# Chunks 6 to 13 of an RWKV-7 scan inverted in blocks of 32 steps and joined on TensorE, with the schedule around it moved

## The chip, the cores and the metric

The kernel runs on one core of a Trainium2 chip. The metric is the device time of one launch in microseconds. Every time given is a median over runs or comes from one profiled execution, and the text says which. The engines are named as the profile names them: PE is the matmul engine and PEld its weight loads, DVE is VectorE, ACT is ScalarE, POOL is GpSimd, SP the engine whose queue issues most DMAs.

## The reference

An RWKV-7 state recurrence over 768 steps, for 4 batches of 8 heads with 40 dimensions each, and on its output a feed-forward layer with a squared ReLU:

```python
for t in range(S):                                   # S = 768
    y[:, :, t] = np.einsum('bhd,bhde->bhe', rt, state)
    Sa = np.einsum('bhde,bhe->bhd', state, at)
    state_decay = state * wt[:, :, None, :] - np.einsum('bhd,bhe->bhde', Sa, bt)
    state = state_decay + np.einsum('bhd,bhe->bhde', vt, kt)
x = y.transpose(0, 2, 1, 3).reshape(B * S, H * D)    # 3072 x 320
h = np.maximum(x @ w_in, 0.0)                        # w_in 320 x 2048
out = h * h @ w_out                                  # w_out 2048 x 320
```

The FFN weights arrive as 64-bit floats; the kernel turns them into 32-bit ones itself.

## The kernel before

The sequence is cut into 24 chunks of 128 steps: chunk i is batch i mod 4, steps 128 (i div 4) onward. A chunk i needs the state that chunk i-4 left, so the chunks form one long sequence with four interleaved chains. Inside a chunk, all steps are solved together, which needs the inverse of a unit lower triangular matrix for each head. A chunk's 128 steps are two halves of 64, and for each half and head a 64 x 64 matrix is inverted; the coupling between the halves is done later with N (`g["N"]`).

The work on a chunk comes in parts, each a Python generator that issues a few instructions and yields:

- `early(i)`, five steps: w, b and a are loaded, turned on PE, the running products of the decay are made on DVE (scans, two reciprocals), b and a are scaled, and their products for all pairs of steps are made on PE. ACT copies these into `N`, and the blocks to be inverted go to DRAM (`kept_q` or `kept_d`, `kept_n`, `kept_m`), with the decays (`kept_e`).
- the inversion, on POOL: `take` loads the blocks of a *unit* of chunks, one block to a partition, and `solve` runs the forward substitution, two POOL instructions a step (L443 and L445). The result goes to DRAM (`kept_t`). Units hold 1, 1, 2, 2, 2, 2, 4, 4, 4 and 2 chunks. Units 0 to 3 (chunks 0 to 5) are "fine": each 64 x 64 matrix is given as two 32 x 32 blocks, 31 steps, and the block below the diagonal is computed on PE. Units 4 to 9 run 63 steps on whole halves.
- `inverses(i)` fetches a chunk's result into the tile `T`. For a coarse unit that is only a load. For a fine one it is the *join*: DVE turns the blocks (`upper_`), ACT spreads them over `T` with the mask `which`, PE makes 16 small products into `mv`, ACT copies them, PE makes 16 more, ACT copies these into `T`. The tiles for this (`mv`, `turned`, `joins`) lie at the end of the FFN's `hidden` buffer, which is free then.
- `rest(i)`, nine steps or more: k, r and v are turned, the masked products A and RV made, the state is brought up to date, and it drives `inverses(i)`.
- `chain(i)`, eleven steps: the part that needs the state of the chunk four before; it ends in a third of a token tile.
- `ffn()`: for each group of three chunks eight up-projection steps (6 matmuls each) and twelve out-projection steps, 160 in all.
- `rounding()`: the pieces of the weights, 10 for the up-projection and 16 for the other, each a few operations on ACT and DVE, out of staging room that lies in `w_out` and in the first 4608 words of `hidden`.

The order on every engine is the order in which the program issues, written out by hand. The start (L750 to L792) prepares chunks 0 to 3. Then come 24 *slots*. Slot i interleaves, in twelve steps (`weave`), chain(i), some steps of the FFN (`share`), the early parts listed for the slot in `ahead`, rest(i+1), and in slots 0 to 4 pieces of weights (`pieces_in`, the number and the step by which they end). What is left of a generator after the twelve steps is issued in one go (`run`), rest last. When all chunks of a unit have had their early part, `take` and `solve` of the unit are issued to POOL at the end of the slot. Unit 4 is stopped after 33 of its 63 steps, and the first part of unit 5's data is loaded before it goes on (`AHEAD`, `EARLIER`).

The schedule before, in numbers: early parts 4 and 5 in slot 0, 6 and 7 in slot 1, 8 and 9 in slot 2, 10 in slot 3, 11 in slot 4, 12 and 13 in slot 5, then one a slot, 17 and 18 in slot 9. The FFN takes 5 steps in slot 4, from its fourth step on, and then up to 7 a slot.

`soon(i)` tells whether the load for chunk i is issued early in `rest(i)`, or late, because its unit has only just been solved:

```python
soon = lambda i: i < 2 * B or unit_of[i - 1] == unit_of[i]      # B = 4
```

Of the kernel before, what the change touches and what calls it, by code (L numbers as in the profile page):

```python
# [17 lines left out]
def kernel(  # L18
# [22 lines left out]
    nc = tc.nc  # L41
# [4 lines left out]
    C = 128  # L46
# [122 lines left out]
    more_rings()  # L169
    x_ = loaded[0] = {nm: fetch(nm, src, 0) for nm, src in (("k", k), ("r", r))}  # L170

    which = single("which", [128, 2])
    nc.gpsimd.memset(which, 0.0)
    for n in range(4):
        nc.gpsimd.memset(which[n * 32:(n + 1) * 32, n % 2:n % 2 + 1], 1.0)

    whole = lambda t_: t_

# [114 lines left out]
    Q = HC // 2  # L293
    kept_e = [dram.tile([USED, 3, NP, C + 2], FP32, tag=f"e{i}", name=f"kept_e{i}") for i in range(len(order))]

    sizes = [1, 1] + [2] * 4 + [4] * ((len(order) - 12) // 4) + [2]
    units = [(sum(sizes[:u]), n) for u, n in enumerate(sizes)]

    FINE = 4
    SMALL = units[FINE][0]  # L300
    kept_q = dram.tile([SMALL, H, 2, 2, Q, Q], FP32, tag="q", name="kept_q")
    kept_m = [dram.tile([2, Q, H, Q], FP32, tag=f"m{i}", name=f"kept_m{i}") for i in range(SMALL)]
# [31 lines left out]
    turned = lambda nm, bufs: new(nm, [128, NP, 128], bufs)  # L334


    def spare(name, i):
        at = NF * GB * C - (("mv", "turned", "joins").index(name) * 2 + i % 2 + 1) * H * Q
        return free_words[:, at:at + H * Q].rearrange("p (h t) -> p h t", h=H)

    def early(i, g=None):

# [43 lines left out]
        if g is None:  # L386
            store(kept_n[i], t_[:HC, :, HC:], 1)
        else:
            g["dec"], g["N"] = dec, new("N21", [HC, H, HC], 2)
            nc.scalar.copy(g["N"], t_[:HC, :, HC:])  # L390
            g["joins"] = spare("joins", i)
            for half in range(2):
                nc.scalar.copy(g["joins"][half * HC:half * HC + Q], joins(half))
        yield
# [5 lines left out]

    part_of = lambda u: given[:, u % 3 * Q * Q:(u % 3 + 1) * Q * Q] if u < FINE else given


    EARLIER = Q * HC

    def take(u, queues, words=slice(None)):
        first, nb = units[u]
        if u < FINE:
            kept = kept_q[first:first + nb].rearrange("b h f k s t -> (b h f k) (s t)")
        else:  # L410
            kept = kept_d[u].rearrange("b h f w -> (b h f) w")
        cols = classes(u)
        rows = 128 // cols
        for col in range(cols):
            queues[col % len(queues)].dma_start(out=part_of(u)[col * rows:(col + 1) * rows, words], in_=kept[:, words])  # L415

    def solve(u, between={}):
        run(solving(u, between))

    def solving(u, between={}, stop=None):  # L420

        first, nb = units[u]
        fine = u < FINE
        size = Q if fine else HC
        cols = classes(u)
        rows = 128 // cols
        part = part_of(u)
        words = size // cols * size
        at = u * Q * Q // 2 if fine else 0
        ts = solved[:, at:at + words]  # L430
        nc.gpsimd.memset(ts, 0.0)
        for col in range(cols):
            nc.gpsimd.memset(ts[col * rows:(col + 1) * rows, col::size + cols], -1.0)
        t3 = ts.rearrange("p (j t) -> p j t", t=size)
        for s in range(size - 1):
            if s in between:
                between[s]()
            if s == stop:
                yield
            n, m_ = s // cols + 1, size - 1 - s  # L440
            at = s * size + s + 1 if s < Q else Q * HC + (s - Q) * (Q + 1) + 1
            p_ = new("half_p", [128, 528], 1)[:, :n * m_].rearrange("p (j t) -> p j t", j=n)
            nc.gpsimd.tensor_tensor(p_, part[:, at:at + m_].unsqueeze(1).to_broadcast([128, n, m_]),  # L443
                                    t3[:, :n, s:s + 1].to_broadcast([128, n, m_]), Alu.mult)
            nc.gpsimd.tensor_tensor(t3[:, :n, s + 1:], t3[:, :n, s + 1:], p_, Alu.subtract)  # L445
        to = kept_t[u]
        to = to.rearrange("n b h f k j t -> (n b h f k) (j t)") if fine else to.rearrange("n b h f j t -> (n b h f) (j t)")
        nc.gpsimd.dma_start(out=to, in_=ts)
# [3 lines left out]
    def inverses(i, g, queue=nc.sync):  # L452
# [13 lines left out]
        if "N" not in g:  # L466
            g["N"] = new("N21", [HC, H, HC], 2)
            queue.dma_start(out=g["N"], in_=kept_n[i])
            if u < FINE:
                g["joins"] = spare("joins", i)  # L470
                for half in range(2):
                    queue.dma_start(out=g["joins"][half * HC:half * HC + Q], in_=kept_m[i][half])
        if u >= FINE:
            return
        yield
        upper_ = spare("turned", i)
        nc.vector.transpose(upper_.rearrange("p h t -> p (h t)"), blocks.rearrange("p h t -> p (h t)"))
        for n in range(2):
            nc.scalar.activation(T[:, :, n * Q:(n + 1) * Q], blocks, Act.Copy, scale=which[:, n:n + 1])
        yield  # L480
        small = lambda: psum(ps_w)[:, :H * Q].rearrange("p (h t) -> p h t", h=H)
        p_ = small()
        mv = spare("mv", i)
        ends_ = [(slice(half * HC, half * HC + Q), slice(half * HC + Q, (half + 1) * HC)) for half in range(2)]
        for h in range(H):
            for one, two in ends_:
                mm(p_[two, h], g["joins"][one, h], upper_[one, h], True)
# [175 lines left out]
    def ffn():  # L663
        for gi in range(len(order) // GB):
# [1 line left out]
                yield False  # L666
            t_ = tokens.pop(gi)
            hid = []
            for f in range(0, NF, 2):
                square(hid[-2:])  # L670
                ps = [psum(ps_f if gi < len(order) // GB - 1 else ps_w)[:, :GB * C] for _ in range(2)]
                for e, p_ in enumerate(ps):
                    half = slice(e * DP, (e + 1) * DP)
                    mm(p_, w_third[half, f * 64:f * 64 + 128], t_[half, NT, :], True)
# [10 lines left out]
            for n in range(GB):  # L685
                bb, c = order[gi * GB + n]
                p_ = psum(ps_f if gi < len(order) // GB - 1 else ps_w)[:, :DM]
                for f in range(NF):
                    mm(p_, hid[f][:, n * C:(n + 1) * C], w_out[:, f], f == 0)
                    if f % PART == PART - 1 and f < NF - 1:  # L690
                        yield True
                o_ = new("o", [128, DM], 2)
# [10 lines left out]
    def run(gen):  # L703
        for _ in gen:
            tick()
# [87 lines left out]


    TOTAL = 12
    ahead = {0: (4, 5), 1: (6, 7), 2: (8, 9), 3: (10,), 4: (11,), 5: (12, 13)}
    ahead.update({i: (i + 8,) for i in range(6, 9)})
    ahead[9] = (17, 18)
    ahead.update({i: (i + 9,) for i in range(10, len(order) - 9)})

    PER, LAG = NF // 2 + 4 * GB, 3
    by_then = [0] * B + [5]
    for i in range(B + 1, len(order)):
        by_then.append(min(by_then[-1] + 7, PER * (i + 1) // GB - PER - LAG if i > 2 * B else PER * i))
    share = {i: (n - (by_then[i - 1] if i else 0), 4 if i == B else 0) for i, n in enumerate(by_then)}
    pieces_in = {0: (4, TOTAL), 1: (6, TOTAL), 2: (6, TOTAL), 3: (7, TOTAL), B: (4, 4)}
    done = set(range(B))
    unit = unit_of[B]

    AHEAD, under_way = (FINE,), []  # L810
    for i in range(len(order)):
        bb, c = order[i]
        n, begin = share[i]
# [16 lines left out]
        weave(*jobs)  # L830
        while unit < len(units) and all(m_ in done for m_ in range(len(order)) if unit_of[m_] == unit):
            flush()
            if under_way:

                take(unit, own, slice(0, EARLIER))
                run(under_way.pop())
                take(unit, own, slice(EARLIER, Q * (HC + Q)))
            else:
                take(unit, own)
            if unit in AHEAD:  # L840
                under_way.append(solving(unit, stop=Q + 1))
                next(under_way[0])
            else:
                solve(unit)
            unit += 1
    flush()
    run(second)
# [30 lines left out]
```

## Time and profile before

| | us |
|---|---|
| median of three runs (lowest, highest) | 1046.84 (1044.67, 1049.31) |
| the profiled execution | 1047.3 |
| its span, from the first to the last instruction | 1045.6 |
| PE busy in the span | 927.4 (89%) |
| POOL busy | 670.6 (64%) |
| DVE busy | 496.8 (48%) |
| ACT busy | 273.0 (26%) |
| mean granted clock of PE | 0.915 of full speed |

The groups of instructions that the change touches, from the profile's list by line, engine and tiles (count, busy us in all, mean ns of one, idle us just before them):

| group | count | busy | mean | idle before |
|---|---|---|---|---|
| POOL L443, product of a step of the substitution | 502 | 298.9 | 595 | 90.2 |
| POOL L445, its subtraction | 502 | 322.4 | 642 | 39.3 |
| PE, first products of the join (into `mv`) | 192 | 5.6 | 222 | 16.6 |
| PE, second products of the join | 192 | 7.3 | 223 | 9.2 |
| ACT L479, blocks spread over T | 12 | 5.4 | 500 | 22.6 |
| ACT L489, copies of mv | 12 | 4.4 | 363 | 1.1 |
| ACT L496, copies into T | 12 | 4.3 | 360 | 5.7 |
| DVE L477, blocks turned | 6 | 2.6 | 438 | 23.4 |

POOL stores the units' results to `kept_t` at 49.0, 76.3, 107.9, 148.0, 251.4, 338.8, 475.1, 609.8, 747.8 and 844.2 us.

How to read it: a stretch of the span is told by the engines' busy time in it. Matmuls are pipelined and their ends modelled, so a PE that is busy is not one at its peak, while a gap on PE is a real wait. "PEclk" is the share of its clock that PE was granted. A releaser is what the waiting instruction's semaphore was last raised by.

### The profile page before, as it was taken

What the parts mean: (1) busy time and instruction counts of PE and PEld (TensorE: products, weight loads), DVE (VectorE), ACT (ScalarE), POOL (GpSimd) and SP (SyncE); (2) the same over time, 40 slices, a digit from 0 to 9 for tenths busy, and PEclk for the clock granted to TensorE, in tenths of its full rate; (3) what the DMA queues carried; (4) which work ended last, traced back from release to release, by engine and by line L of the source; (5) the groups of instructions that cost most, each with busy time, mean ns of one, the idle gap of its engine ahead of it and who ended that gap; (6) DMA issues with size and microseconds to landing.
All of it is one profiled execution on the core that took longest, in us unless ns stands there. A gap on an engine that the chain in (4) does not pass through costs nothing.

```text
span 1045.6 us, 19803 instructions
## 1 busy us (share of the span) xinstructions
PE 927.4 (89%) x7824; PEld 672.1 (64%) x7824; DVE 496.8 (48%) x940; ACT 273.0 (26%) x627; POOL 670.6 (64%) x1128
## 2 busy tenths in 40 slices
PE   6364665688999999997999999999999999999998
PEld 5253455576667766775677766775677567756656
DVE  5556685796554465453744545534432432222120
ACT  3132332334332133122232132113212311232020
POOL 4778454897898599995999949999668820000000
PEclk8656676667999999998999999999999999999999
DMA  8987989688184938198564596064425432520000
GB/s 108 154 145 146 178 196 179 163 158 147 43 137 92 193 55 136 24 164 194 61 113 90 87 183 119 21 118 59 115 50 98 66 72 49 98 30 7 23 0 19
DMA packets 260360, 106.92 MB, mean 102 GB/s; under 512 B 243724, under 2 KB 249356, under 8 KB 258604
## 3 DMA queue, kind: packets, MB, share of 16 engines
q1 hardware_dynamic: 255740, 86.65, 47.8%
q0 software_dynamic: 3440, 18.88, 7.8%
q8 instruction: 62, 1.02, 0.4%
q10 hardware_dynamic: 1088, 0.13, 0.1%
q14 instruction: 30, 0.25, 0.1%
HBM read 72.47 MB, written 31.19 MB: 99 GB/s over the span
## 4 chain that ended last, share of the span: by engine, by line
PE 52%; POOL 28%; DMA 10%; issue 5%; DVE 2%; ACT 2%; SPq 1%; POOLq 0%; DVEq 0%; ACTq 0%
PE ps_f L87 26%; POOL half_t L445 14%; POOL half_p L443 13%; PE ps_w L87 11%; PE ps_c L87 10%; DMA half_n<-kept_d 3%; PE ps_w L314 2%; DMA kept_t<-half_t 1%; DMA half_n<-kept_q 1%; DMA in_w<-in_w_dram 1%; DMA T<-kept_t 1%; DMA w_out<-in_moe_w_in_dram 1%; PE ps_w L542 1%; DMA kept_m<-N 1%; POOL half_n L415 1%
## 5 line engine op out<-in xcount | busy, mean ns | idle before, releaser
L443 POOL TENSOR_TENSOR half_p<-half_n,half_t 128x70 f32<-128x70 f32 (+52 forms) x502 | 298.9, 595 | 90.2 <-DMA half_n<-kept_d 39.8
L445 POOL TENSOR_TENSOR half_t<-half_t,half_p 128x70 f32<-128x70 f32 (+52 forms) x502 | 322.4, 642 | 39.3
L87 PE MATMUL ps_f<-w_out,hid 128*128 128x320 f32 x672 | 198.6, 440 | 0.0
L87 PE MATMUL ps_f<-tokens,w_in 128*128 128x384 f32 x448 | 162.3, 506 | 0.0
L661 DVE TENSOR_TENSOR hid<-hid 128x384 f32<-128x384 f32 x128 | 94.4, 752 | 139.4 <-ACT hid L679 139.0
L87 PEld LDWEIGHTS ps_f<-w_out,hid 128*128 128x128 f32 x672 | 121.6, 190 | 44.9 <-issue 2.1
L87 PEld LDWEIGHTS ps_f<-tokens,w_in 128*128 128x128 f32 x448 | 82.1, 193 | 77.2 <-issue 33.8
L679 ACT ACTIVATE hid<-ps_f 128x384 f32<-128x384 f32 x112 | 54.9, 490 | 201.1 <-PE ps_f L87 201.1
L330 DVE TENSOR_TENSOR A<-ps_w,upper 128x512 f32<-128x512 f32 x48 | 30.9, 686 | 108.0 <-PE ps_w L87 108.0
L87 PE MATMUL ps_w<-decay,bT 40*128 40x128 f32 x352 | 31.7, 330 | 33.2 <-DVE decay L360 29.5
L514 DVE TENSOR_TENSOR kvT<-ps_w,dec 128x512 f32<-128x512 f32 x24 | 16.5, 687 | 88.7 <-DMA dec<-kept_e 46.6
L87 PE MATMUL ps_f<-tokens,w_third 64*128 64x384 f32 x224 | 55.4, 540 | 0.0
L87 PEld LDWEIGHTS ps_w<-decay,bT 40*128 40x128 f32 x352 | 26.9, 229 | 41.8 <-DVE decay L360 26.7
L87 PE MATMUL ps_c<-xr,T 64*64 64x40 f32 x768 | 39.1, 242 | 13.7 <-ACT xr L592 6.7
L351 DVE TENSOR_TENSOR_SCAN decay<-ps_w,ones 128x64 f32<-128x64 f32 x88 | 23.8, 270 | 54.2 <-PE ps_w L314 54.1
L87 PEld LDWEIGHTS ps_c<-xr,T 64*64 64x64 f32 x768 | 32.5, 148 | 25.1 <-ACT xr L592 13.1
L330 DVE TENSOR_TENSOR RX<-ps_w,upper 128x512 f32<-128x512 f32 x48 | 30.8, 683 | 26.2 <-PE ps_w L87 25.9
L330 DVE TENSOR_TENSOR RV<-ps_w,upper 128x512 f32<-128x512 f32 x48 | 30.9, 686 | 18.1 <-PE ps_w L87 17.9
L355 DVE RECIPROCAL decay<-decay 128x256 f32<-128x256 f32 x22 | 38.3, 1739 | 0.0
L356 DVE RECIPROCAL decay<-decay 128x256 f32<-128x256 f32 x22 | 37.3, 1694 | 0.0
L87 PE MATMUL ps_w<-rT,xnT 40*128 40x128 f32 x384 | 34.2, 293 | 2.4 <-ACT rT L524 2.4
L524 ACT COPY rT<-ps_w 128x512 f32<-128x512 f32 x24 | 14.0, 585 | 82.5 <-PE ps_w L314 82.5
(139 smaller groups left out, 1391.0 us busy)
## 6 DMA issues: line engine op xcount, KB each, us to landing
kept_e<-decay SPq DMA_DIRECT2D x22, 633.8 KB
dec<-kept_e SPq DMA_DIRECT2D x22, 633.8 KB
hid<-in_moe_w_out_dram SPq DMA_DIRECT2D x16, 320.0 KB
half_n<-kept_d POOLq DMA_DIRECT2D x6, 768.0 KB, 11.4
in_w<-in_w_dram SPq DMA_DIRECT2D x24, 160.0 KB
in_ab<-in_b_dram SPq DMA_DIRECT2D x24, 160.0 KB
in_ab<-in_a_dram SPq DMA_DIRECT2D x24, 160.0 KB
in_k<-in_k_dram SPq DMA_DIRECT2D x24, 160.0 KB
```

What stands on the lines that cost most here:

```text
L87: nc.tensor.matmul(o, l_, r_, start=start, stop=True, skip_group_check=True)
L314: nc.tensor.transpose(p_[:, q * 128:(q + 1) * 128], pair(x_, q), ident)
L330: nc.vector.tensor_tensor(t_, p_, over4(upper), Alu.mult)
L351: nc.vector.tensor_tensor_scan(up[:, q, MID + 1:C + 1], wT[:, q, MID:], ones, 1.0, Alu.mult, Alu.mult)
L355: nc.vector.reciprocal(down[:, :, MID + 1:C + 1], up[:, :, MID + 1:C + 1])
L356: nc.vector.reciprocal(up[:, :, :MID], down[:, :, :MID])
L443: nc.gpsimd.tensor_tensor(p_, part[:, at:at + m_].unsqueeze(1).to_broadcast([128, n, m_]), t3[:, :n, s:s + 1].to_broadcast([128, n, m_]), ...
L445: nc.gpsimd.tensor_tensor(t3[:, :n, s + 1:], t3[:, :n, s + 1:], p_, Alu.subtract)
L514: nc.vector.tensor_tensor(kT, kT_, down[:, :, 1:C + 1], Alu.mult)
L524: nc.scalar.copy(rT, turn(x_["r"]))
L661: nc.vector.tensor_tensor(h_, h_, h_, Alu.mult)
L679: nc.scalar.activation(h_, p_, Act.Relu)
```

## The change

Units now hold 1, 1, 2, 2, 2, 2, 2, 2, 4, 4 and 2 chunks, and the first eight (chunks 0 to 13) are fine, so chunks 6 to 13 are inverted in blocks of 32 too and joined on PE. For these the join's off-diagonal inputs are stored by `early` (`kept_m`, now of 14 chunks) and loaded straight into the half of `T` that the join's result later overwrites. `T` is filled by one scaled copy and two plain ones. A tile of its own, `turned_blocks`, holds the turned blocks and then the products `mv`, so that the joins of later chunks no longer lie in the FFN's buffer. The split of unit 4 (`AHEAD`) is gone. Early parts: one a slot in slots 1 to 4, two a slot in slots 5 to 8, one from slot 9 on. The FFN takes two steps in slot 3, in its last three steps; its first group goes through the up-projection's tiles in the order 12 to 15, 0 to 11, since the other parts of `hidden` still hold staged weights, and uses the PSUM pool `ps_w` while pieces are left. Slot 2 takes one weight piece more, slot 3 one fewer, and those end by its ninth step.

```diff
-    sizes = [1, 1] + [2] * 4 + [4] * ((len(order) - 12) // 4) + [2]
+    sizes = [1, 1] + [2] * 6 + [4] * ((len(order) - 16) // 4) + [2]
-    FINE = 4
+    FINE = 8
...
-    def spare(name, i):
-        at = NF * GB * C - (("mv", "turned", "joins").index(name) * 2 + i % 2 + 1) * H * Q
+    def spare(i):
+        at = NF * GB * C - (i % 2 + 1) * H * Q
...
+    turned_blocks = single("turned_blocks", [128, H, Q])
...
             if u < FINE:
-                g["joins"] = spare("joins", i)
+
+                g["joins"] = T[:, :, Q:]
                 for half in range(2):
                     queue.dma_start(out=g["joins"][half * HC:half * HC + Q], in_=kept_m[i][half])
...
-        upper_ = spare("turned", i)
+        upper_ = mv = turned_blocks
         nc.vector.transpose(upper_.rearrange("p h t -> p (h t)"), blocks.rearrange("p h t -> p (h t)"))
-        for n in range(2):
-            nc.scalar.activation(T[:, :, n * Q:(n + 1) * Q], blocks, Act.Copy, scale=which[:, n:n + 1])
+        ends_ = [(slice(half * HC, half * HC + Q), slice(half * HC + Q, (half + 1) * HC)) for half in range(2)]
+        nc.scalar.activation(T[:, :, :Q], blocks, Act.Copy, scale=which)
+        for _, two in ends_:
+            nc.scalar.copy(T[two, :, Q:], blocks[two])
         yield
...
-            for f in range(0, NF, 2):
+
+            for f in range(-4 if gi == 0 else 0, NF - 4 if gi == 0 else NF, 2):
+                f %= NF
                 square(hid[-2:])
-                ps = [psum(ps_f if gi < len(order) // GB - 1 else ps_w)[:, :GB * C] for _ in range(2)]
+                ps = [psum(ps_w if left() or gi == len(order) // GB - 1 else ps_f)[:, :GB * C] for _ in range(2)]
...
-    ahead = {0: (4, 5), 1: (6, 7), 2: (8, 9), 3: (10,), 4: (11,), 5: (12, 13)}
-    ahead.update({i: (i + 8,) for i in range(6, 9)})
-    ahead[9] = (17, 18)
-    ahead.update({i: (i + 9,) for i in range(10, len(order) - 9)})
+    ahead = {0: (4, 5), 1: (6,), 2: (7,), 3: (8,), 4: (9,), 5: (10, 11), 6: (12, 13), 7: (14, 15), 8: (16, 17)}
+    ahead.update({i: (i + 9,) for i in range(9, len(order) - 9)})
...
-    by_then = [0] * B + [5]
+    by_then = [0] * (B - 1) + [2, 7]
...
-    share = {i: (n - (by_then[i - 1] if i else 0), 4 if i == B else 0) for i, n in enumerate(by_then)}
-    pieces_in = {0: (4, TOTAL), 1: (6, TOTAL), 2: (6, TOTAL), 3: (7, TOTAL), B: (4, 4)}
+    share = {i: (n - (by_then[i - 1] if i else 0), {B - 1: 9, B: 4}.get(i, 0)) for i, n in enumerate(by_then)}
+    pieces_in = {0: (4, TOTAL), 1: (6, TOTAL), 2: (7, TOTAL), 3: (6, 9), B: (4, 4)}
...
-            if under_way:
-
-                take(unit, own, slice(0, EARLIER))
-                run(under_way.pop())
-                take(unit, own, slice(EARLIER, Q * (HC + Q)))
-            else:
-                take(unit, own)
-            if unit in AHEAD:
-                under_way.append(solving(unit, stop=Q + 1))
-                next(under_way[0])
-            else:
-                solve(unit)
+            take(unit, own)
+            solve(unit)
             unit += 1
```

The mask `which` loses its second column, `solving` becomes `solve` without its stop, and the out-projection names its operand `hidden[:, f]` instead of `hid[f]`, for the order of the first group.

## The prediction

> **What bounds the kernel now.** I read the page first: busy shares, then its forty slices of 26.1 us, then the chain that ended last.
>
> ```profile
> PE   6364665688999999997999999999999999999998
> ...
> POOL 4778454897898599995999949999668820000000
> PEclk8656676667999999998999999999999999999999
> DMA  8987989688184938198564596064425432520000
> ```
>
> PE is the busiest engine from slice 9 on (235 us) and its granted clock is near full there. Before that PE is at 30 to 70%, the clock at 0.5 to 0.8, and the DMA engines at 80 to 90%. So there are two regimes: a start in which PE is starved, and from about 240 us a stretch in which PE is full. POOL's digits are high in both.
>
> ```profile
> PE 52%; POOL 28%; DMA 10%; issue 5%; DVE 2%; ACT 2%; SPq 1%; POOLq 0%; DVEq 0%; ACTq 0%
> ...
> L87 PE MATMUL ps_f<-w_out,hid 128*128 128x320 f32 x672 | 198.6, 440 | 0.0
> ```
>
> POOL has 28% of the chain (the inversions), but a chain share says what came last, not what a shorter POOL is worth: in its stretch PE is full as well. To see which, I cut the span by slots. Slot i starts where chunk i's first small copy out of PSUM (L583) starts; slots 1 to 5 and 10 follow. The columns are the stretch, its length, busy us (instructions) of PE, PEld, DVE, ACT, POOL, then clock, DMA share, GB/s.
>
> ```profile
> core 0: us, PE busy (x) PEld busy (x) DVE busy (x) ACT busy (x) POOL busy (x), PEclk, DMA share, GB/s
> 105.40:154.90 49.50, 30.25 (x321) 25.18 (x320) 37.99 (x70) 17.07 (x39) 27.05 (x76) 0.67 0.96 185
> 154.90:204.90 50.00, 31.16 (x320) 26.89 (x320) 32.58 (x71) 15.38 (x39) 31.56 (x64) 0.64 0.86 169
> 204.90:241.00 36.10, 29.54 (x312) 25.54 (x312) 31.37 (x68) 15.09 (x36) 32.40 (x53) 0.65 0.84 162
> 241.00:288.90 47.90, 43.93 (x382) 30.30 (x384) 27.51 (x55) 15.71 (x38) 39.23 (x84) 0.86 0.52 93
> 288.90:329.20 40.30, 39.78 (x353) 29.01 (x354) 24.77 (x47) 11.64 (x28) 35.99 (x56) 1.00 0.59 97
> 479.60:530.60 51.00, 45.32 (x342) 29.53 (x344) 27.03 (x43) 13.39 (x31) 40.84 (x51) 0.93 0.73 134
> ```
>
> Slots 1 and 2 take 50 us with two early parts each and PE busy 30 to 31 us of them; slot 3 takes 36.1 us with one. Their clock is 0.64 to 0.67. Slot 1's DMA engines are busy for 96% of it at 185 GB/s. From slot 5 on PE is busy for 39.8 us of 40.3. So time can be gained only ahead of slot 5, or at an exception later. What stops PE in slots 1 to 3:
>
> ```profile
> PE ps_w L87 <- DVE decay L360: 14.9, 4, 6.1
> PE ps_w L314 <- DMA in_w<-in_w_dram: 11.2, 2, 7.9
> PE ps_w L314 <- DMA in_k<-in_k_dram: 4.9, 1, 4.9
> ```
>
> The first two are the early parts' own latencies (the decay products, and w that arrives late), the third an input of the next chunk. The one exception after slot 5 is slot 10, where PE waits for unit 6's inverse (chunks 10 to 13), which POOL stored at 475.1 us:
>
> ```profile
> 483.49 0.60 PE L314 MATMUL ps_w<-ident,in_w 128*128 128x128 f32 x4
> 489.53 1.08 PE L87 MATMUL ps_c<-xr,T 64*64 64x40 f32 x16 [5.44 <-DMA T<-kept_t]
> ```
>
> **What the Trainium skill says.** "TensorE: Matmul & The Clock Gate", section "Part 1: The HAM clock gate", says that the array's clock is halved after a quiet window of about 3.4 us and restored after a busy one; the trace agrees: slots 1 to 3 average 0.64 to 0.67, slots 5 to 9 are at 1.00, and the 5.4 us gap in slot 10 pulls it to 0.93. The same page, "Step-by-step: what each phase is for", says that matmuls keep program order, so a matmul that waits holds all behind it: the join below shows that. "SBUF — State Buffer", "Who interferes with whom", says that a VectorE instruction with two SBUF inputs contends with GpSimd reading SBUF; the square of L661 averages 831 ns from 480 to 840 us and 554 ns from 850 us, when POOL is done. It helps VectorE, which is not the bound.
>
> **The change, part by part**, against the profiled execution: 1047.3 us, of which the span is 1045.6; that is 0.5 above the median of the runs.
>
> *POOL.* Units 4 to 6 now occupy it from 157.9 to 475.1 us, 317 us. Four units of the short kind replace them. Such a one (unit 2) runs from its memset at 76.9 to its store at 107.9: 31 us, plus some 10 us of load wait, so 4 x 41 = 164 us. They can start when chunks 7, 9, 11 and 13 are made, at the ends of slots 2, 4, 5 and 6, some three slots before each is wanted. The two units of four then have slack too (134 us for unit 7, wanted in slot 14). POOL leaves the path. Worth: the gap of 5.4 us in slot 10, and its clock: 0.07 x 51 us = 3.5 us of full clock lost. Gain 8.8 us (5.4 if the clock's share is not real). The rest of POOL's saving lies beside full PE: nothing.
>
> *Early parts spread (6 in slot 1, 7 in 2, 8 in 3, 9 in 4).* Slots 1 and 2 lose one each. Slot 1 is DMA-bound:
>
> ```profile
> kept_e<-decay SPq DMA_DIRECT2D x22, 633.8 KB
> ...
> in_w<-in_w_dram SPq DMA_DIRECT2D x24, 160.0 KB
> ...
> kept_d<-N SPq DMA_DIRECT2D x36, 64.0 KB
> ```
>
> An early part moves three inputs of 160 KB, 633.8 of kept_e, 128 of kept_n and 192 of kept_d, 1.43 MB, 7.8 us at 185 GB/s. So slot 1: 49.5 - 7.8 = 41.7; with a little less waiting, 41 (from 36.1, as slot 3 is, to 45): -8.5. The new kept_m stores are 64 KB a chunk, 0.3 us. Slot 2 loses this and also the 1.5 MB that POOL fetches for unit 4 (four loads of 384 KB), 8.5 - 2.9 = 5.6 MB, 30 us at that rate, so DMA no longer binds; it becomes like slot 3: 36.5 us (34 to 41), with one weight piece more: -13.5. Slots 3 and 4 keep one early part. The two parts come back in slots 6 to 8 (net), in full PE: 12 transposes and 16 products, 1.0 + 0.5 + 1.1 = 2.6 us at full clock by the trace at 261 to 281 us: +5.2.
>
> *FFN from slot 3.* Two steps move there from slots 15 and 18 (the running sums of the schedule meet again there), where PE is full: a warm step takes 3.6 us (257.45 to 260.98), so -7.2 there. In slot 3 they go into its last two steps. The first step of slot 4, at half clock, took 6.5 us (248.3 to 254.8); PE's 1.1 us wait there is filled. I take +6 (4 if the array is warm, 11 if not and PSUM's buffers are short). Pieces squeezed into nine steps: hidden, VectorE has 5 us free in slot 3. Slot 4: -0.5 (+-3).
>
> Start in sum: -8.5 - 13.5 + 6 - 0.5 = -16.5 (from -27 to 0).
>
> *Joins.* Eight more chunks (6 to 13) are joined on PE, in slots 5 to 12, all full. What one costs there is seen at the end of slot 4, already at full clock:
>
> ```profile
> 280.74 1.16 PE L87 MATMUL ps_w<-decay,bT 40*128 40x128 f32 x16
> 281.83 0.69 PE L87 MATMUL ps_w<-hid 32*32 32x32 f32 x32
> 284.13 1.08 PE L87 MATMUL ps_w<-blocks,hid 32*32 32x32 f32 x32 [1.60 <-ACT hid L489]
> 285.14 1.98 PE L87 MATMUL ps_c<-A,in_v 128*64 128x128 f32 x16
> ```
>
> From the early part's last product to the next chunk's first product: 281.83 to 285.14 = 3.3 us. Of it 0.69 and 1.0 are matmuls; 1.6 PE waits for ACT, which has the early part's three kinds of N copy ahead of the two mv copies. The second half is issued right behind the first, when the slot's interleaving is over, so nothing lies between them to cover it. 8 x 3.3 = 26.4 (14 if the wait were covered, 50 if the blocks' loads came late too). For chunks 8, 10 and 12, the first of their units, "soon" is false: the fills of T come in the last step, 0.5 + 2 x 0.36 = 1.2 us of ACT just ahead of the mv copies: 3 x 1.2 = 3.6 (0 to 9). And a pause of low activity may drop the clock: the next chunk's A product after this join took 1.98 us, against 1.09 at 477.5 us. I count half of the joins at 1.7 us lost: 6.8 (0 to 14). Extra stores and loads on SP's queue, four a chunk at most, lie beside PE-bound slots; behind them wait the next chunk's k, dec and r, asked for a slot ahead: nothing, unless they are late. ACT's extra 2.7 us a slot lies in slots where it is busy 9 to 16 us.
>
> Late part in sum: 26.4 + 3.6 + 6.8 + 5.2 - 7.2 - 8.8 = +26.0. With the start: +9.5, 1056.8; less 0.5 for the median, 1056.
>
> **Rivals.**
> *A, forecast, 0.52:* PE is full, and what PE gets to do (joins) outweighs the idle time taken out of the start: 1056.
> *B, faster, 0.22:* the cold start shrinks all the way. Slots 1 and 2 become 36.1 us each (-27.3), slot 3 costs 4, and no join drops the clock or adds a fill: -23.3 + 26.4 + 5.2 - 7.2 - 8.8 = -7.7, 1039. For it: slot 3 shows that length with one early part. Against: 185 GB/s in slot 1. It decides once slots 1 and 2 together take under about 77 us.
> *C, no change, 0.18:* start -21, late +21: 1047.
> *D, far slower, 0.08:* the joins' loads (blocks, and joins that need T's buffer) come late behind SP's other DMAs, and PE stands 3 us more for each: +24, 1080. For it: the DMA wait for the T load at 480.5 us was 8.9 us; against: these loads are issued three steps or more ahead.
>
> That the inverses still come from POOL late would undo the slot 10 gain alone: 1065, inside A's range.
>
> **How the numbers follow.** A measurement here tells 0.5%, 5.2 us, from no change. A and D are slower: 0.60; C 0.18; B 0.22. A's own range, from its terms, is 1048 to 1072; down to B and up towards D, 1036 to 1074 leaves out about 2 in 10.
>
> **What would show it.** Right: slots 1 and 2 near 41 and 37 us; PE's wait for T in slot 10 gone; eight gaps of 1.5 us or more before the second join matmuls in slots 5 to 12, slots there 3 to 5 us longer with the same FFN steps; half-clock windows behind some. Wrong: those gaps filled, or slots 1 and 2 under 77 us together (B); waits for DMA at the joins (D); POOL still in the chain after 300 us.

## The result, and the profile after

| | before | after |
|---|---|---|
| median of four runs each on the same chip (lowest, highest), us | 1048.07 (1044.67, 1052.46) | 1084.87 (1083.85, 1088.12) |
| after over before, with 95% interval | | 1.0354 (1.0307 to 1.0401) |
| span of the profiled execution, us | 1045.6 | 1082.0 |
| PE busy, us | 927.4 | 955.8 |
| POOL busy, us | 670.6 | 508.4 |
| mean granted clock of PE | 0.915 | 0.904 |

The kernel is slower by 37 us. The forecast, 1056, had the sign and missed the size: the time lies above its range, which ended at 1074. The page of the kernel after, its forty slices and its chain of waits (line numbers are now those of the kernel after; POOL's two instructions are L437 and L439, the first small copy of a slot is L578):

```profile
PE   6373678589998998998999899999999999999998
...
POOL 4788440350273662019999316999868810000000
PEclk9665556588999899989999999999999999999999
DMA  9878975925568685584533835637154412430000
...
PE 75%; DMA 7%; DVE 6%; ACT 5%; issue 3%; POOL 3%; SPq 1%; DVEq 0%; POOLq 0%; ACTq 0%
```

POOL now has holes (counting the slices from 1, digits of 0 to 2 in slices 7, 10, 11, 16 to 18 and 24) and 3% of the chain instead of 28%, none of it after 58 us. PE has 75% of the chain. But PE's own row, which read 9 almost throughout from slice 11 on, now has 8s among the 9s up to slice 23, and so has its clock row up to slice 21. To see where the time went I cut the span by slots again (stretch, length, busy us and instructions of PE, PEld, DVE, ACT and POOL, clock, DMA share, GB/s). Slots 1 to 5 of the kernel after:

```profile
core 0: us, PE busy (x) PEld busy (x) DVE busy (x) ACT busy (x) POOL busy (x), PEclk, DMA share, GB/s
106.40:151.60 45.20, 30.07 (x292) 25.65 (x292) 32.33 (x58) 16.09 (x35) 26.25 (x74) 0.54 0.82 164
151.60:186.70 35.10, 28.85 (x292) 24.50 (x292) 28.70 (x63) 15.21 (x36) 0.00 (x0) 0.60 0.70 132
186.70:240.70 54.00, 37.65 (x336) 29.23 (x336) 30.04 (x67) 16.83 (x39) 25.64 (x68) 0.67 0.59 122
240.70:288.30 47.60, 43.05 (x382) 29.39 (x384) 25.50 (x55) 16.08 (x38) 1.47 (x3) 0.89 0.45 67
288.30:330.40 42.10, 39.50 (x409) 30.22 (x409) 21.28 (x44) 12.51 (x30) 23.76 (x66) 0.98 0.78 132
```

Against the kernel before, slot 1 fell from 49.5 to 45.2 us and slot 2 from 50.0 to 35.1. Slot 3 rose from 36.1 to 54.0, and in it PE is busy for only 37.7 us. So slot 5 starts at 288.3 us, where it had started at 288.9: what the start gained is gone before the stretch in which PE is full begins. From there the kernel falls behind. Slots 5 to 13 take 397.8 us (288.3 to 686.1) instead of 356.6 (288.9 to 645.5), and what follows slot 14's start takes 395.9 instead of 400.1.

*Slot 3.* The waits of all engines in slot 3 of the kernel after (what waited, for what; us in all, times, longest):

```profile
DVE kvT L509 <- DMA dec<-kept_e: 9.9, 1, 9.9
...
PE ps_w L314 <- DMA in_k<-in_k_dram: 8.7, 1, 8.7
```

The next chunk's k and its decays `dec` come 9 to 10 us late. The issues of SP's queue there show why (start, us taken by the group, what is moved, how many):

```profile
178.32 7.58 SPq L108 DMA_DIRECT2D tokens<-tokens  x8
186.02 0.43 SPq L108 DMA_DIRECT2D kept_e<-decay  x1
186.57 0.39 SPq L247 DMA_DIRECT2D hid<-in_moe_w_out_dram  x1
187.05 3.30 SPq L108 DMA_DIRECT2D kept_q<-N  x2
190.40 0.64 SPq L108 DMA_DIRECT2D kept_m<-N  x1
191.09 1.09 SPq L108 DMA_DIRECT2D kept_q<-N  x2
192.22 0.69 SPq L108 DMA_DIRECT2D kept_m<-N  x1
193.00 0.56 SPq L108 DMA_DIRECT2D kept_n<-N  x1
193.66 0.57 SPq L247 DMA_DIRECT2D hid<-in_moe_w_out_dram  x1
194.32 0.40 SPq L142 DMA_DIRECT2D in_k<-in_k_dram  x1
```

Slot 3 starts at 186.7 us, and SP reaches the load of k only at 194.32, behind the tail of slot 2's stores. In the kernel before the same load came ahead of slot 3, which started at 204.9:

```profile
190.36 6.32 SPq L108 DMA_DIRECT2D tokens<-tokens  x8
...
203.54 0.40 SPq L142 DMA_DIRECT2D in_k<-in_k_dram  x1
```

The token stores had begun 14.5 us ahead of slot 3 then, and now begin 8.4 us ahead. Slot 2 became shorter; the work of SP's queue at its end did not. Slot 1 shows the same (SP issues its k at 110.3 us, 3.9 us into the slot, and PE waits 5.7 us for it).

*Slots 5 to 13.* PE's waits in 288 to 645 us of the kernel after, and one of its joins, that of chunk 10, in the timeline of PE and then of ACT (start, us, what; in brackets the idle time before it and what ended it):

```profile
PE ps_w L87 <- ACT turned_blocks L484: 17.4, 8, 3.0
...
PE ps_w L314 <- DMA in_w<-in_w_dram: 0.7, 1, 0.7
```

```profile
506.34 0.69 PE L87 MATMUL ps_w<-turned_blocks,T 32*32 32x32 f32 x32
510.00 1.45 PE L87 MATMUL ps_w<-blocks,turned_blocks 32*32 32x32 f32 x32 [2.96 <-ACT turned_blocks L484]
511.38 1.98 PE L87 MATMUL ps_c<-A,in_v 128*64 128x128 f32 x16
```

```profile
506.44 0.58 ACT L370 COPY N<-ps_w 128x512 f32<-128x512 f32 x1 [0.59 <-PE ps_w L87]
507.05 0.76 ACT L374 COPY N<-ps_w 64x256 f32<-64x256 f32 x2
507.83 0.37 ACT L375 COPY N<-ps_w 64x256 f32<-64x256 f32 x1
508.22 0.51 ACT L474 ACTIVATE T<-blocks,which 128x256 f32<-128x256 f32 x1
508.74 0.82 ACT L476 COPY T<-blocks 32x256 f32<-32x256 f32 x2
509.58 0.75 ACT L484 COPY turned_blocks<-ps_w 32x256 f32<-32x256 f32 x2
```

Each of the eight joins stops PE once, for the two copies of `mv` (L484), which stand on ACT behind the early part's copies of N and, in chunks 8, 10 and 12, behind the fills of T as well. In five of the eight joins the next chunk's A product already runs at half clock, as here (1.98 us, where the joins of chunks 6, 11 and 13 have 1.1). In two more the clock falls just behind it, and one join, that of chunk 11, keeps it. The waits for DMA, which would have been rival D, are 0.7 us in all.

### The profile page after: what moved, and what is told of

It reads as the page before. It is cut to its first block, busy times and chain, and to the rows that moved or that the text cites. A ratio compares the mean times of both kernels' runs of the same rounds, so it can differ in the third digit from the quotient of the medians.

```text
span 1082.0 us, 20823 instructions
## 1 busy us (share of the span) xinstructions
PE 955.8 (88%) x8336; PEld 695.0 (64%) x8336; DVE 485.5 (45%) x948; ACT 298.5 (28%) x689; POOL 508.4 (47%) x990
## 4 chain that ended last, share of the span: by engine, by line
PE 75%; DMA 7%; DVE 6%; ACT 5%; issue 3%; POOL 3%; SPq 1%; DVEq 0%; POOLq 0%; ACTq 0%
PE ps_f L87 35%; PE ps_c L87 16%; PE ps_w L87 16%; PE ps_w L314 4%; DMA dec<-kept_e 3%; POOL half_t L439 1%; POOL half_p L437 1%; PE ps_w L537 1%; DMA kept_e<-decay 1%; ACT turned_blocks L484 1%; PE ps_c L612 1%; PE ps_c L547 1%; DVE decay L358 1%; ACT xr L587 1%; DMA w_out<-in_moe_w_in_dram 1%
## 5 line engine op out<-in xcount | busy, mean ns | idle before, releaser
L437 POOL TENSOR_TENSOR half_p<-half_n,half_t 128x126 f32<-128x126 f32 (+44 forms) x437 | 223.1, 511 | 103.6 <-DMA half_n<-kept_q 41.1
L439 POOL TENSOR_TENSOR half_t<-half_t,half_p 128x126 f32<-128x126 f32 (+44 forms) x437 | 240.2, 550 | 34.2
L87 PE MATMUL ps_f<-tokens,w_in 128*128 128x384 f32 x432 | 155.8, 504 | 0.0
L656 DVE TENSOR_TENSOR hid<-hid 128x384 f32<-128x384 f32 x128 | 81.8, 657 | 125.5 <-ACT hid L676 125.5
L87 PEld LDWEIGHTS ps_f<-tokens,w_in 128*128 128x128 f32 x432 | 78.6, 192 | 75.2 <-issue 33.0
L415 POOL DMA_DIRECT2D half_n<-kept_q x18 | 9.4, 528 | 124.0 <-DMA kept_q<-N 76.2
L509 DVE TENSOR_TENSOR kvT<-ps_w,dec 128x512 f32<-128x512 f32 x24 | 16.5, 689 | 104.9 <-DMA dec<-kept_e 55.8
L415 POOL DMA_DIRECT2D half_n<-kept_d x8 | 4.0, 506 | 94.0 <-DMA kept_d<-N 93.9
L87 PEld LDWEIGHTS ps_c<-xr,T 64*64 64x64 f32 x768 | 32.6, 149 | 20.5 <-ACT xr L587 13.6
L87 PE MATMUL ps_w<-decay,bT 40*128 40x128 f32 x352 | 28.2, 303 | 19.8 <-DVE decay L363 19.8
L87 PE MATMUL ps_w<-blocks,turned_blocks 32*32 32x32 f32 x448 | 16.8, 221 | 31.9 <-ACT turned_blocks L484 30.3
L87 PE MATMUL ps_w<-rT,kvT 40*128 40x128 f32 x384 | 33.9, 310 | 7.0 <-DVE RX L330 5.8
```

What stands on the lines that cost most here:

```text
L87: nc.tensor.matmul(o, l_, r_, start=start, stop=True, skip_group_check=True)
L509: nc.vector.tensor_tensor(kT, kT_, down[:, :, 1:C + 1], Alu.mult)
L656: nc.vector.tensor_tensor(h_, h_, h_, Alu.mult)
```

## The experiments

Two theories stood at first for the 41 us that slots 5 to 13 lost: the joins at the slots' ends (J), or the loads and the order of SP and ACT around them (L). For slot 3 there were the FFN's two steps and the late loads. All ratios are against the kernel before on the same chip, with 95% intervals. The column "slots 1 to 4" and the others are from each run's one profiled execution. Slot 0, which the edits of the experiments leave alone, differs by up to 4.4 us between those executions, so the slots are compared and not the moments at which they start.

| run | median us | ratio | slot 2 | slot 3 | slots 1 to 4 | slots 5 to 13 | PE idle in 5 to 13 |
|---|---|---|---|---|---|---|---|
| before | 1048.07 | 1 | 50.0 | 36.1 | 183.5 | 356.6 | 9.0 |
| after | 1084.87 | 1.0354 (1.0307 to 1.0401) | 35.1 | 54.0 | 181.9 | 397.8 | 23.0 |
| e1_joins_off | 1055.90 | 1.0055 (1.0030 to 1.0081) | 35.9 | 52.8 | 179.1 | 372.7 | 16.0 |
| e2_ffn_slot4 | 1085.12 | 1.0321 (1.0289 to 1.0353) | 35.5 | 46.4 | 172.5 | 401.7 | 22.6 |
| e3_load_first | 1084.34 | 1.0308 (1.0274 to 1.0341) | 35.8 | 53.3 | 181.0 | 398.2 | 22.2 |
| e4_join_early | 1064.46 | 1.0126 (1.0100 to 1.0152) | 35.1 | 54.5 | 182.2 | 377.6 | 9.7 |
| e5_load_sooner | 1080.77 | 1.0329 (1.0282 to 1.0375) | 36.2 | 51.1 | 177.1 | 399.3 | 22.1 |
| e6_early_joins_sooner_loads | 1049.20 | 1.0000 (0.9980 to 1.0020) | 35.1 | 52.1 | 180.0 | 368.9 | 5.9 |
| e7_joins_old_schedule | 1089.30 | 1.0392 (1.0368 to 1.0416) | 47.3 | 38.8 | 183.6 | 396.7 | 21.4 |
| e8_before_sooner_loads | 1044.70 | 0.9965 (0.9952 to 0.9979) | 42.2 | 36.2 | 172.6 | 362.8 | 14.4 |
| e9_one_unit_joined | 1043.65 | 0.9939 (0.9919 to 0.9958) | 42.6 | 36.7 | 176.0 | 359.0 | 7.0 |
| e10_filled_gap | 1079.59 | 1.0273 (1.0236 to 1.0311) | 36.3 | 54.2 | 182.3 | 391.5 | 5.7 |
| e11_spread_sooner_no_ffn | 1084.63 | 1.0320 (1.0285 to 1.0356) | 36.2 | 44.2 | 173.5 | 403.9 | 23.2 |

### The joins left out

For chunks 6 to 13 the join's products and their copies are left out; the loads and fills of T stay.

```diff
+        if i >= 6:
+            yield
+            yield
+            return
         p_ = small()
         for h in range(H):
```

> Leaves out the two sets of join products on PE and their four ACT copies for chunks 6 to 13 (the off-diagonal quarter of their T is then not computed); loads, transposes and fills of T stay. Theory J (the loss after slot 5, 37 us, is the joins on PE: matmuls 1.7, wait 1.6 or more, and a half-clock window behind each): slots 5 to 13 lose 8 x 5 = 40 us, the half-clock windows there vanish, and the time is 1045 (1038 to 1052). Theory L (the loss is the extra loads and early parts moved into slots 6 to 8, that is DMA and VectorE order): only the bare matmul time goes, 8 x 1.7 = 14 us, 1071, and gaps and half-clock windows stay.

The kernel lost 29 us of its 1084.87: about four fifths of what the change costs. That is between the two theories and nearer J. Slots 5 to 13 took 372.7 us, 25 less. They are not back at 356.6, since waits that the joins had covered now show, with 20.5 us at half clock behind them (PE in slots 5 to 12 of this run):

```profile
PE ps_w L314 <- DMA in_r<-in_r_dram: 4.9, 1, 4.9
PE ps_w L314 <- DMA in_k<-in_k_dram: 4.0, 2, 3.4
PE ps_w L314 <- DMA in_w<-in_w_dram: 3.7, 1, 3.7
```

So removing the joins uncovers 12.6 us of late inputs, and each theory holds a part.

### The FFN's two steps put back

```diff
-    by_then = [0] * (B - 1) + [2, 7]
+    by_then = [0] * B + [5]
```

> The FFN begins in slot 4 again, with 5 steps; all else as changed. Theory F (slot 3's 54 us, 18 over before, come from the two FFN steps and their PSUM buffers): slot 3 falls to 38 to 42, 7 us come back in slots 15 and 18, 1076 to 1080. Theory S (slot 3 waits for the k and decay loads of chunk 4, which stand on SP's queue behind the flushed stores and a weight fetch that waits for DVE): slot 3 keeps its 8.7 us wait for k and falls by 4 to 8 us only, to 46 to 50; with the 7 back, 1083 to 1088, no change.

Slot 3 fell by 7.6 us, to 46.4. The whole did not move. The two steps came back: slots 5 to 13 took 3.9 us more and the rest after slot 14's start 4.3 us more (400.2 against 395.9). The early FFN is neutral. Ten of slot 3's 18 us are not the FFN: with it gone PE still stands for 16.8 us in slot 3, against 6.6 before the change, and waits 5.7 us for k.

### The loads asked for sooner, first attempt

```diff
         weave(*jobs)
+        if i == 2:
+            ready[4] = {}
+            load(4, ready[4])
...
-            if i:
+            if i and i + 1 not in ready:
                 ready[i + 1] = {}
```

> The loads of chunk 4's k, decays and r are issued on SP at the end of slot 2, ahead of the stores and the weight fetch that are flushed there. Theory S: the waits for k (8.7 us, PE) and the decays (9.9 us, DVE) in slot 3 go or shrink to 2 us, slot 3 becomes 46 us, the whole 1077. Theory F: slot 3 stays at 52 or more, 1083 to 1086.

This run tells nothing. The loads of k and `dec` were asked for after the whole of slot 2 had been issued, its leftovers included, so the stores stood ahead of them as they had: SP issued k at 194.16 us, where it had been 194.32.

### The joins inside the slot

The products of the join of chunks 6 to 13 are issued between other steps of `rest`, not one behind the other at its end, so that other matmuls lie between the first products, the copies and the second.

```diff
+        sooner = i >= 6 and unit_of[i] < FINE
-        if soon(i):
+        if soon(i) or sooner:
             next(joining, None)
...
         g["rT"] = rT
+        if sooner:
+            next(joining)
         yield
...
-        if i and unit_of[i] < FINE:
+        if i and unit_of[i] < FINE and not sooner:
             next(joining)
...
         inv = p_.rearrange("t (h d) -> t h d", h=H)[:, :, :D]
+        if sooner:
+            next(joining)
         yield
...
+        if sooner:
+            next(joining)
         yield
         yield from joining
```

> For chunks 6 to 13 the join is issued inside the slot's interleaving: loads two steps after the start of rest, transposes with rT, first products with the turned decays, second products with the scaled k and b, so that FFN and chain work stands between them on PE. Theory J with its wait and clock as part: the 1.6 us gaps and the half-clock windows go, 8 x (1.6 + 1.5) = 25 us, 1060 (1052 to 1066). If only the matmuls themselves count: no change, 1082 to 1086. If the loads come too late for the earlier place: ACT waits for the blocks, FFN copies behind it, slower than 1085.

The median fell by 20 us, slots 5 to 13 by the same 20. The two longest of PE's waits in slots 5 to 12 of this run:

```profile
PE ps_w L314 <- DMA in_v<-in_v_dram: 3.2, 1, 3.2
PE ps_w L314 <- DMA in_w<-in_w_dram: 3.0, 1, 3.0
```

The 17.4 us of waits for `turned_blocks` are gone with no product left out; 6.2 us for inputs took a part of their place. Leaving the joins out had taken 25 us off these slots, and moving them takes 20. What the joins cost is therefore mostly where they stand and not their matmuls.

### The loads asked for sooner, second attempt

A hook issues chunk 4's loads between the twelve steps of slot 2 and the run of its leftovers, ahead of the last stores.

```diff
-    def weave(*gens):
+    def weave(*gens, after=None):
...
+        if after:
+            after()
         for gen, _, _, _ in gens:
             run(gen)
...
+        def next_loads():
+            ready[i + 2] = {}
+            load(i + 2, ready[i + 2])
-        weave(*jobs)
+        weave(*jobs, after=next_loads if i == 2 else None)
```

> Chunk 4's k, decays and r are issued on SP inside slot 2, ahead of the stores of early part 7 and the last weight fetch (seven issues, from 187 to 194 us in the changed kernel). The edit of the run before had left SP's order as it was. Theory S (slot 3's wait for k and the decays is SP's queue, whose tail behind the end of slot 2 is as long as before while the slot is 15 us shorter): the loads are issued at 187, the waits for k (8.7) and decays (9.9) fall by 6 to 7 us, slot 3 becomes 47 to 49 and the whole 1078 to 1081. Rival D (the load itself is slow, because the DMA engines are full): the waits move by 2 us at most, 1083 to 1087.

SP now issues k at 184.38 us, just as slot 3 starts (184.4), where it had been 7.6 us into the slot. PE's waits in slot 3 of this run:

```profile
PE ps_w L87 <- DVE bT L362: 4.0, 1, 4.0
PE ps_w L314 <- DMA in_k<-in_k_dram: 2.3, 1, 2.3
```

The wait for k went from 8.7 to 2.3 us, DVE's wait for `dec` from 9.9 to 1.5, and slot 3 from 54.0 to 51.1, short of the 47 to 49 that were expected. A wait for the early part's `bT` on DVE has taken its place. So the late load is real, and behind it lies the early part's own latency, little shorter. The medians lie 4 us apart, as expected, but their intervals overlap, so only the slot decides.

### Joins inside, loads sooner in every slot

The edit of e4 and the hook of e5 for all slots from 1 on.

> The joins of chunks 6 to 13 inside the interleaving, as in the run that gave 1064, and each slot's loads of k, decays and r ahead of the stores of the slot before. If both losses are the ones named (joins at the end of a slot, inputs late on SP): 1064 less 7 in slot 3, less 3 in slot 1, less some 6 in slots 6 and 9, 1048 (1042 to 1054), no worse than before. If sooner loads only push the stores back that POOL waits for: 1060 or more.

1049.20 against 1048.99 for the kernel before: no difference. With the joins' place and the loads mended, the change is level with the kernel before as it stood. The hook alone makes that kernel faster too, though (1044.70, two runs further down, on the same chip; the two intervals lie just apart), so beside a kernel before with the same hook the change still costs some 4.5 us. Slots 5 to 13 still take 12.3 us more than before, and slots 1 to 4 3.5 less.

### The joins with the schedule of before

The kernel after with the early parts, the FFN's steps and the weight pieces of before (`ahead`, `by_then`, `pieces_in`).

> Joins for chunks 6 to 13 as in the change, but early parts, FFN's start and weight pieces as in the kernel before. Theory J: slots 1 to 4 as before, slots 5 to 12 lose 8 x (3.3 + 1.7) less what slot 10's wait gave, so 1048 + 40 - 9 = 1079 (1072 to 1084); the new schedule is then worth about -6, nearly nothing. Rival L (the moved early parts make the loss): 1055 to 1062.

1089.30, above what was expected: the joins, with the units that go with them, cost 40 us without the new schedule (slots 5 to 13: 396.7, +40.1), and the new schedule is worth some 4 us, if anything: the two intervals overlap.

### The hook alone on the kernel before

> The kernel before with the loads of k, decays and r of each slot ahead of the stores at the end of the slot before. Slot 2 and the late slots have hardly a wait for k there (4.9 and 0.6 us), so if SP's order hurts only short slots: 1044 to 1050, no change. If it hurts throughout: under 1040.

No change was expected, and it was a small gain: 0.9965. Slot 2 fell from 50.0 to 42.2 us and slots 1 to 4 by 10.9. What went in slot 2 is not a wait for k, of which it had none: PE had waited 7.9 us there for w, the early part's input, and no longer does. More than half of it is lost again in slot 10 (57.0 us, from 51.0), now reached sooner than POOL is done with unit 6 (stored at 468 us); PE there waits

```profile
PE ps_c L87 <- DMA T<-kept_t: 10.8, 1, 10.8
```

where it had waited 5.4 us. So late loads were there before the change too, and mending them makes POOL the next bound.

### One unit joined

With the schedule and units of before, only unit 4 (chunks 6 and 7) is made fine, its joins inside the slot, the loads sooner: sizes of before, `FINE = 5`, no split unit, the edit of e4, the hook.

> A version meant to beat both: schedule and units of the kernel before, but unit 4 (chunks 6 and 7) alone solved in blocks of 32 and joined inside the interleaving, no split of unit 4, and each slot's loads of k, decays and r ahead of the stores of the slot before. The run with sooner loads alone gave 1044.7 and now waits 11 us in slot 10 for unit 6 (stored at 468 us, wanted about 10 us sooner). If POOL is what holds slot 10: unit 4 takes some 40 us less of POOL, unit 6 starts when chunk 13 is made, about 318 us, and is stored by 450 us; the wait and the half-clock stretch behind it go (11 + 6), two covered joins cost 4: 1032 (1028 to 1037). If unit 6 is still late, or the joins cost as at a slot's end: 1042 or more.

1043.65 us, the fastest here and faster than both kernels (0.9939), but 1032 was expected. The wait in slot 10 is gone (43.9 us instead of 57.0), as it should. But the two joins and the unsplit unit gave back 7.4 us in slot 6 (41.6 us against 34.2 in e8), among it

```profile
PE ps_w L87 <- DVE RX L330: 3.5, 1, 3.5
```

with 3.4 us at half clock after it, and some 2 us each in slots 4 and 5. Its interval still overlaps that of e8, so the two can't be ranked.

### The gap filled

To price the clock alone, five large matmuls whose result nobody reads are put between the join's two sets of products, in chunks 6 to 13.

```diff
             nc.scalar.copy(mv[two], p_[two])
+        if i >= 6:
+            warm_ = psum(ps_w)[:, :GB * C]
+            for _ in range(5):
+                mm(warm_, w_in[:, 0, :128], w_in[:, 0, :GB * C], True)
         yield
```

> The changed kernel with five matmuls of 128x384, whose result nobody reads, between the two sets of join products of chunks 6 to 13: they fill PE's wait of about 2 us and leave it there. Theory C (half of a join's cost is the clock halved behind the gap): the half-clock windows in slots 5 to 13, 34 us in the changed kernel, go, worth up to 17 us: 1072 (1068 to 1077), though PE does more work. Rival G (the gap and the matmuls are the cost, the clock a by-product): 1084 to 1090.

Measured 1079.59, between the two expectations, because both took the filling to fit into the gap. The timeline of PE in this run, at the join of chunk 10, shows that it does not:

```profile
503.68 0.69 PE L87 MATMUL ps_w<-turned_blocks,T 32*32 32x32 f32 x32
504.31 3.49 PE L87 MATMUL ps_w<-w_in 128*128 128x384 f32 x10
507.73 0.69 PE L87 MATMUL ps_w<-blocks,turned_blocks 32*32 32x32 f32 x32
508.35 1.09 PE L87 MATMUL ps_c<-A,in_v 128*64 128x128 f32 x16
```

The filling holds PE for 3.42 us (504.31 to 507.73) in every join, 27.4 us in all, where the eight gaps had been 17.4. It adds 10.0 us. Still slots 5 to 13 became 6.3 us shorter, and their clock is 0.98 to 1.00. So the half clock behind the eight joins cost 10.0 + 6.3 = 16.3 us. A second count agrees: slots 5 to 13 of the kernel after have 34.1 us at half clock, half of which is 17.1, and this run keeps 1.7 us, half of which is 0.9; that leaves 16.2. The medians lie only 5.3 us apart and their intervals touch; the slots decide, since 397.8, 398.2 and 399.3 us in the three runs with the same joins (after, e3, e5) stand against 391.5.

### Loads sooner and no early FFN

> The changed kernel with the FFN from slot 4 and chunk 4's loads ahead of the stores in slot 2. The FFN steps were worth 8 us of slot 3 and the loads 3 to 4. If they add: slot 3 is 42 us, of which 36 would be as in the kernel before; the whole 1080 (FFN's 7 us come back late). If the steps hid behind the wait: slot 3 stays at 46, 1084.

e2 and e5 together. Slot 3 is 44.2 us, 2.2 less than in e2, and the whole is where it was. PE waits 4.5 us there for DVE's `decay` (L363), 2.7 for k and 2.8 for the two `turned_blocks` copies of the join. In slot 3 the two gains nearly add up: 9.8 us, of 7.6 and 2.9. In the whole nothing of them is left: slots 5 to 13 take 6.1 us more than in the kernel after.

## Why the prediction was right in sign and wrong in size

**Right: PE is the bound, and work moved to PE shows.** POOL left the path as costed: it has no part in the chain after 58 us, slot 10's wait for T is gone, and VectorE's square (L656) became quicker with POOL's pauses, 752 to 657 ns on average, worth nothing here, as the prediction said. Slots 1 and 2 took 80.3 us together, above the 77 from which rival B decides, and the forecast had 77.5. Rival C fell. Rival D's 1080 is close to the time, but its mechanism, DMA waits at the joins, is not there.

**Wrong, the start: "-16.5" was -1.6 (slots 1 to 4: 183.5 to 181.9).** Slot 2's "-13.5" measured -14.9 and slot 4's "-0.5" -0.3; slot 1's "-8.5" was only -4.3. The mis-sized term is slot 3's "+6", which measured +17.9. The FFN's steps in it were near their price (7.6). The other 10 are idle PE. They come from a step costed at nothing: the prediction wrote of SP's queue that behind the stores "wait the next chunk's k, dec and r, asked for a slot ahead: nothing, unless they are late". They aren't asked for a slot ahead. `load(i + 1)` is called at the head of slot i, and `rest(i + 1)` turns k in its second step, in the same slot. The prediction even showed a wait of 4.9 us for k (it is in slot 1), without asking what lay ahead of that load in SP's queue. Slot 2 lost 15 us of its length, its stores lost little, and the load met their tail. e5 shows that the load is late for that reason and that asking sooner takes 6.4 us off the wait for k and 8.4 off that for `dec`; e5 and e11 show also that only 2 to 3 us of it reach the slot, since DVE's part of the early work is late next. How the rest of the 10 us divides between the early part's latency and the other inputs isn't settled. Slot 1, at "41", is 45.2, with 5.7 us of the same wait for k; it was 42.8 to 45.4 in the runs with one early part there.

**Wrong, the late part: "+26.0" was +37.0** (slots 5 to 13 +41.2, after them -4.2). By terms:

| term, us | forecast | measured | from |
|---|---|---|---|
| PE idle: joins' waits 12.8, fills 3.6, slot 10's gap -5.4 | +11.0 | +14.0 | idle of slots 5 to 13, 9.0 to 23.0 |
| matmuls of the joins (13.6) and of the two early parts (5.2) | +18.8 | +17.8 | busy +27.5, less the clock (+13.6), plus the FFN's 3.9 |
| clock: joins 6.8, slot 10 -3.4 | +3.4 | +13.6 | half of the time at half clock, 6.8 to 34.1 us |
| FFN's two steps gone from there | -7.2 | -8.2 | e2 |
| sum | +26.0 | +37.2 | |

The matmuls' line is what is left when the others are taken out, so the sum closes of itself. The same working on e6, where the joins stand inside the slot, gives 18.6 (busy +15.4, less 0.7 for the clock, plus the FFN's 3.9). The joins' place and their wait for ACT were foreseen: 17.4 us of waits in eight gaps against 16.4. The term that failed is the clock: "I count half of the joins at 1.7 us lost: 6.8 (0 to 14)". Seven of the eight joins lost it, three of them for twice as long (6.8 us at half clock, not 3.4), ten half windows and not four. The Trainium skill, "TensorE: Matmul & The Clock Gate", section "HAM oscillation — how this bites in real kernels", prices a stretch at half clock at half its length; the 34 us here at half clock would cost 17 by it, and e10 measured 16.3. The price per window was right, the number of windows was not; what decides whether a join loses one is in the last section.

**A condition of its own: the joins' cost depends on where they stand.** The prediction noted that nothing lies between the two halves of a join to cover the wait. e4 and e10 show that this and the clock make up most of it: filling the gap with matmuls that the kernel needs anyway takes 20 us off. What the joins then still cost is mainly their products, 13.6 us by the forecast's price, which no run measures alone.

## What to carry to other kernels

When a change shortens a stretch, look at the in-order queue of DMA issues across the stretch's end: stores that had time to drain there become a delay for the first load behind them, and the gain of one stretch is lost in the next. Find the place in the code where each load is issued, and the last issues ahead of it in the trace, before costing a queue at nothing. When a chain matmul, copy, matmul is put into a full PE, put it where other matmuls lie between its halves; at a stretch's end it costs its wait and the clock after it, here more than its own work.

## What the hardware showed beyond that

PE's clock fell behind gaps shorter than its window. The Trainium skill, "TensorE: Matmul & The Clock Gate", section "HAM oscillation — how this bites in real kernels", gives as an abstract rule no idle gaps over about 3.4 us; here gaps of 1.6 to 3.0 us were followed by one or two windows of 3.4 us at half clock in seven joins of eight. Around each gap stand only 32x32 products, and when the gap was filled with full-size matmuls (e10) the clock stayed up.

What decides can be read from the traces. In each of the thirteen, all changes of the clock lie on one grid of 3.41 us. Four stretches of that grid in the kernel after, two at the join of chunk 10 (a gap of 2.96 us) and two at the join of chunk 11 (1.60 us):

```profile
core 0: us, PE busy (x) PEld busy (x) DVE busy (x) ACT busy (x) POOL busy (x), PEclk, DMA share, GB/s
506.18:509.59 3.41, 0.85 (x37) 0.62 (x34) 0.33 (x1) 3.00 (x8) 3.17 (x4) 1.00 0.20 41
509.59:513.01 3.42, 2.93 (x48) 2.67 (x48) 0.00 (x0) 1.44 (x4) 3.19 (x4) 0.50 0.75 134
553.97:557.38 3.41, 2.84 (x53) 2.01 (x51) 1.67 (x2) 1.11 (x3) 3.25 (x3) 1.00 0.14 46
557.38:560.79 3.41, 2.23 (x54) 1.91 (x56) 0.00 (x0) 2.02 (x6) 3.17 (x4) 1.00 0.40 80
```

At chunk 10 PE was busy for 0.85 us of a window, and the next ran at half clock. At chunk 11 the pause is split over two windows, and the clock stayed up; in e2, e7 and e11 the same join, with the same gap, left PE busy for 1.66 to 2.10 us of one window and lost it. From 25 us into slot 4 to 30 us before the end, the thirteen traces have 2827 windows at full clock. Behind those in which PE was busy for 2.04 us or less (60) the next was at half clock, but for one (1.46 us, in e9); behind those with 2.33 us or more (2752) it never was; between the two it was in 9 of 15. Matmuls' ends are modelled, so the limit can't be told more sharply. The small products are not needed for it: in e6 a gap of 2.10 us between a full-size product of the FFN and 40x128 products left 1.20 us of its window busy, and 6.8 us at half clock followed. In the kernel after's three joins that lost two windows, PE was busy for 2.8 to 3.3 us of the first of them; in the four that lost one, for all of it.

Filling the gaps with useless work paid: 27.4 us of matmuls that nobody reads, 10.0 more than the gaps had been, bought back 16.3 us of clock.
